# Two decode layers on one core: FFN weights packed at the turn, column sums moved, kept scores split with ScalarE, outputs scaled on ScalarE, y copied in parts

## The chip, the core and the metric

One core of a Trainium2 chip runs the whole program. Its engines run side by side, each its own instructions in order: TensorE (PE), VectorE (DVE), ScalarE (ACT) and GpSimd (POOL). SyncE (SP) only issues loads from the chip's main memory into the on-chip arena. PE writes its results to a small memory of its own, from which DVE and ACT read. The metric is device time in microseconds (us); lower is better.

## What is computed

Two equal layers, each attention over a long cache and then a gated FFN, for two sequences and one new token each. D = 448, 16 heads of 256, 4096 cached keys, F = 1792, all float32:

```python
def _A_ref(x, k_cache, v_cache, wq, wo):
    q = (x @ wq).reshape(B, Sq, H, Dh).transpose(0, 2, 1, 3)
    scores = einsum("bhqd,bhkd->bhqk", q, k_cache) * (Dh ** -0.5)
    o = einsum("bhqk,bhkd->bhqd", softmax(scores), v_cache)
    return o.transpose(0, 2, 1, 3).reshape(B, Sq, H * Dh) @ wo
def _B_ref(x, W_gate, W_up, W_down):
    gate = x @ W_gate
    return (gate * (gate > 0) * (x @ W_up)) @ W_down

x = A_x
x = x + _A_ref(_layernorm(x), k_cache, v_cache, wq, wo)
x = x + _B_ref(_layernorm(x), W_gate, W_up, W_down)
x = x + _A_ref(_layernorm(x), k_cache, v_cache, wq, wo)
x = x + _B_ref(_layernorm(x), W_gate, W_up, W_down)
```

Both layers use the same weights and the same cache. Nearly all the work is reading keys and values: 32 pairs of head and sequence, each with 4 MiB of keys and 4 MiB of values, in each layer.

## The kernel before

**Units.** A unit `u` is one pair of head and sequence; 32 of them make an attention. Its 4096 keys lie as 32 tiles of 256 columns over 128 partitions, loaded in up to four chunks of eight tiles (1 MiB). The main loop of `attention` goes over `u` and handles the scores of unit `u`, the weighting of values of unit `u - 1`, and the output of unit `u - 2`, in an order that is written out by hand; nothing reorders it. So each engine has one fixed list of instructions.

**Scores** (`score`, `score_block`). Where a unit's keys came in one piece, DVE multiplies all 32 tiles by the query in one instruction (L378) and sums each tile in another (L386). In units 25 to 28 of the first layer and 25 to 29 of the second, ACT sums the first eight tiles (L382) and DVE the other 24. Where keys came in chunks, DVE and ACT share them chunk by chunk (L409, L411, L415), or DVE multiplies and sums one tile in one fused instruction (L418). Then POOL finds the maximum over the partitions (L429), ACT takes the exponentials (L434, L437).

**Values and output.** `weigh` (L462) is 16 PE matmuls for a unit. `out_copy` (ACT, L475) and `out_add` (DVE, L478) fold the result, `out_turn` (PE, L488) turns it, `out_keep` (DVE, L501) divides it by the softmax sums, for both sequences of a head at once in odd units, and `project` (PE, L511) multiplies by wo. On DVE, `out_keep` of unit `u - 2` stands behind three of the four chunks of the scores of unit `u`. The scoring query of a new head (`query`, L309 to L342) stands on PE behind `project`.

**Kept keys.** The second layer goes through the heads in another order and begins with the last two heads of the first. The keys of units 29, 30 and 31 of the first layer, and the values of 30 and 31, are therefore loaded once and kept: their scores in the first layer may not overwrite them, so L418 writes its products to a tile that nobody reads, `junk` (part of `down`). ACT has no part in them.

**Loads.** The arena holds 27 units of 1 MiB: three blocks of eight, and three singles for weights. `pump` issues the loads of a list, `pending`, strictly in order on SP, as soon as a place is free; `release` frees a place and calls `pump`. A load of a list that has no place holds back all behind it. SP waits with each for the engines that used the place last, and for the eighth load before it.

**The turn.** Between the two attentions lies `ffn(False)`: `absorb` adds the attention's result to x, `proj` multiplies by the seven pieces of w_in (L576; pieces 0 to 3 for the gate, 3 to 6 for the other half), `block` by the four of w_out (L669). Each piece of w_in has 1792 columns and takes a unit of 2048. Between pieces 4 and 5, PE computes column sums of the next query weights (`between`, L596 to L606) for the next layer's first query, which is put together without waiting for the layernorm. `busy` issues matmuls that nobody reads, so that PE isn't idle in short waits; `FILL` says where. `ffn(True)` is the same at the end, with the output y gathered in PE's memory (`y_left`, and `y_end` for the last 64 columns), copied at L702 and L710, and sent by SP (L703) and ACT (L711).

Of the kernel before, what the change touches and what calls it, by code (L numbers as in the profile page):

```python
# [15 lines left out]
P = 128  # L16
# [7 lines left out]
PAIR = 2 * NC  # L24
WHOLE_FIRST = range(1, 28)
WHOLE_SECOND = range(9, 29)
KEPT = 20
ALONE = 25
# [11 lines left out]
class Arena:  # L40


    def __init__(self):
        self.free = set(range(BLOCKS * PAIR + SINGLES))

    def take(self, n, kind, after=None):


        split = {}
        for size in (2, NC, PAIR):  # L50
            for i in range(0, BLOCKS * PAIR, size):
                if all(k in self.free for k in range(i, i + size)):
                    split |= {k: size for k in range(i, i + size)}
        found = sorted(self.free, key=lambda k: (split.get(k, 1), k))
# [11 lines left out]
        self.free -= set(range(found[0], found[0] + n))  # L66
# [4 lines left out]
def two_layers(  # L71
# [20 lines left out]
    arena = consts.tile([P, (BLOCKS * PAIR + SINGLES) * UNIT], F32, name="arena")  # L92
# [9 lines left out]
    def source(key, n):  # L102
# [6 lines left out]
        if kind == "h":  # L109
            return w_head[name]  # L110
        if kind == "in":
            return w_in[c]
        return w_out[:, 14 * P * c : min(14 * P * (c + 1), 14 * D)]

    def pump():
        while pending:
            (kind, name, c), n = pending[0]
            last = at_of.get((kind, name, c - 1)) if kind in "kv" else None
            at = units.take(n, kind, last)
            if at is None:  # L120
                return
            pending.pop(0)
            src = source((kind, name, c), n)
            dst = arena[:, at * UNIT : at * UNIT + src.shape[1]]
# [7 lines left out]
            for k in range(n):  # L132
# [3 lines left out]
                at_of[key] = at + k  # L136
# [3 lines left out]
    def get(*key):  # L140
        at = at_of[key]
        return arena[:, at * UNIT : (at + 1) * UNIT]

    def release(*key):
        units.free.add(at_of.pop(key))
        pump()
# [46 lines left out]
    pending += of_first + [(key, 1) for key in ffn_loads]  # L193
# [4 lines left out]
    junk = down[:, :DH]  # L198
    y_end_row = row[SUMS : SUMS + B, D:]
# [41 lines left out]
    def busy(n):  # L241
# [6 lines left out]
        )  # L248

# [45 lines left out]
    def attention(order, after, q_first=None, begun=None):  # L295
# [74 lines left out]
        def score_block(u, c):  # L370


            at = at_of["k", order[u], 0] * UNIT
# [5 lines left out]
            shared = 0 if (WHOLE_SECOND if ahead else WHOLE_FIRST)[0] <= u < ALONE else CT  # L379
# [11 lines left out]
        def score(u, c):  # L391
# [24 lines left out]
            else:  # L416
                for t in range(whole, CT):
                    nc.vector.scalar_tensor_tensor(  # L418
# [26 lines left out]
        def softmax_sum(u):  # L445
# [4 lines left out]
            nc.vector.reciprocal(r_of[u - 1], total)  # L450

        def weigh(u, c):
# [3 lines left out]
            if (u - n_u, c) in FILL:  # L456
# [37 lines left out]

        def out_keep(u):
            if u % 2 == 0:
                return
            h = order[u][0]
            oT_of[h] = work.tile([P, 2, B], F32, name="oT")
            share = r_of.pop(u - 1)[:, None, :].to_broadcast([P, 2, B])  # L500
            nc.vector.tensor_mul(oT_of[h], pT_of.pop(u - 1), share)  # L501
# [58 lines left out]
    def ffn(last):  # L560
# [5 lines left out]
        if not last:  # L566
            h, b = second[0]
            w_q = get("h", h, 0)

        def proj(parts):  # L570

            p = ps_f.tile([P, D], F32, name="pf")
            for n, (part, c, done) in enumerate(parts):
                w = get("in", "", part)
                for j in range(4):
                    nc.tensor.matmul(  # L576
                        p[32 * j : 32 * j + 32, :],
                        xs[:, c, :32],
                        w[:, j * D : (j + 1) * D],
# [3 lines left out]
                if done:  # L583
                    release("in", "", part)
                if part in (4, 5):
# [3 lines left out]
        def between(part):  # L589
# [4 lines left out]
            elif part == 4:  # L594
                for c in range(2):
                    nc.tensor.matmul(  # L596
                        cols, ones.to_broadcast([P, P]), w_q[:, c * DH : (c + 1) * DH],
                        start=(c == 0), stop=False,
                    )
            else:  # L600
                nc.tensor.matmul(
                    cols, ones.to_broadcast([P, P]), w_q[:, 2 * DH : FULL * DH],
                    start=False, stop=False,
                )
                for j in range(2):
                    nc.tensor.matmul(  # L606
                        cols[:, j * P : (j + 1) * P],
# [227 lines left out]
```

## Time and profile before

| | |
|---|---|
| median of 3 runs | 1320.69 us (1320.47 to 1320.93) |
| the profiled execution: its own time | 1320.27 us |
| its span | 1318.5 us |
| loads | 562.56 MB, 427 GB/s over the span |
| busy: DVE, PE, POOL, ACT | 82%, 42%, 20%, 15% |
| mean clock that PE was granted | 0.68 |

The span goes from the first to the last instruction of the profiled execution; 1.8 us of its time lie around it. Rows of a timeline begin with the start (us from the span's start) and the duration, then engine, line, operation and operands; in brackets stands how long the engine sat idle before and what ended that. In rows of groups, "x51 | 443.3, 8692" is 51 instructions, 443.3 us together and 8692 ns each. SPq and ACTq are the queues that issue transfers. Line numbers are those of the kernel before unless a row names the changed one.

### The profile page before, as it was taken

The page shows a single profiled execution, that of the slowest core. Times are in us where ns is not written, and L with a number is a line of the kernel's source. Part 1 is how long each engine was busy: PE and PEld are TensorE (multiplying, and loading weights), DVE is VectorE, ACT ScalarE, POOL GpSimd, SP SyncE. Part 2 cuts the span into 40 slices and gives each one's busy share as a digit, 9 for nine tenths or more (in the row PEclk, how much of TensorE's full clock was granted, in tenths as well). Part 3 has the DMA queues.
Part 4 walks back from the last instruction along what each step waited for, and adds up shares of the span by engine and source line. Part 5 has one row for each costly group of instructions (what it writes and reads, how often), then busy time and mean ns, then how long its engine had stood idle before and what let it go on. Part 6 is the DMA issues. An engine that isn't in the chain of part 4 may idle for free.

```text
span 1318.5 us, 9085 instructions
## 1 busy us (share of the span) xinstructions
PE 553.7 (42%) x3276; PEld 190.6 (14%) x3276; DVE 1081.6 (82%) x780; ACT 195.6 (15%) x776; POOL 269.0 (20%) x192
## 2 busy tenths in 40 slices
PE   2243342433434324345585444242433424434348
PEld 2011010110111101112141111110111101101113
DVE  4989888898888988888729987798888988877892
ACT  2100000000000000212026513000000000012241
POOL 0002003322133220321001153030123331230210
PEclk9675666656667667666697777666767667666679
DMA  9999999999999999999999999999999999999998
GB/s 408 435 430 429 432 428 437 432 436 434 417 445 435 430 430 426 445 418 430 421 405 416 431 430 435 438 432 430 432 431 436 433 428 436 429 432 425 427 425 334
DMA packets 22665, 563.16 MB, mean 427 GB/s; under 512 B 2520, under 2 KB 2652, under 8 KB 9564
## 3 DMA queue, kind: packets, MB, share of 16 engines
q1 hardware_dynamic: 22612, 562.57, 99.5%
q8 instruction: 26, 0.43, 0.1%
q14 instruction: 19, 0.16, 0.0%
q10 hardware_dynamic: 8, 0.00, 0.0%
HBM read 562.56 MB, written 0.00 MB: 427 GB/s over the span
## 4 chain that ended last, share of the span: by engine, by line
DMA 55%; DVE 32%; PE 7%; POOL 2%; issue 2%; ACT 1%; DVEq 0%; SPq 0%; POOLq 0%; ACTq 0%
DMA arena<-in_vk_dram 54%; DVE arena L378 12%; DVE scores L386 11%; DVE arena L409 3%; DVE down L418 2%; PE po L462 2%; POOL top L429 2%; DVE arena L418 2%; DMA arena<-in_w_out_dram 1%; DVE row L478 1%; PE small L488 1%; PE acc L511 1%; DVE scores L415 1%; ACT arena L411 1%; PE pf L576 1%
## 5 line engine op out<-in xcount | busy, mean ns | idle before, releaser
L378 DVE TENSOR_TENSOR arena<-arena 128x8192 f32<-128x8192 f32 x51 | 443.3, 8692 | 111.0 <-DMA arena<-in_vk_dram 110.9
L386 DVE TENSOR_REDUCE scores<-arena 128x32 f32<-128x8192 f32 (+1 forms) x53 | 431.8, 8148 | 0.0
L488 PE MATMUL small<-ones,row 128*128 128x1 f32 x256 | 62.0, 346 | 686.3 <-DVE row L478 686.3
L462 PE MATMUL po<-arena,probs 128*2 128x512 f32 x2048 | 303.1, 734 | 10.3 <-DMA arena<-in_vk_dram 6.6
L429 POOL PARTITION_ALL_REDUCE top<-mx x64 | 64.6, 1009 | 645.8 <-DVE mx L427 645.8
L443 POOL PARTITION_ALL_REDUCE total<-rs x64 | 176.1, 2752 | 61.3 <-ACT probs L437 60.3
L488 PEld LDWEIGHTS small<-ones,row 128*128 128x128 f32 x256 | 56.5, 308 | 748.9 <-DVE row L478 748.9
L434 ACT ACTIVATE nm<-top,nsr 128x1 f32<-128x1 f32 x64 | 18.8, 294 | 612.4 <-POOL top L429 612.4
L354 POOL PARTITION_BROADCAST arena<-arena x58 | 27.6, 545 | 300.6 <-ACT arena L350 300.6
L462 PEld LDWEIGHTS po<-arena,probs 128*2 128x2 f32 x2048 | 54.8, 96 | 198.3 <-issue 191.2
L338 PE MATMUL pq<-arena,xs 128*33 128x256 f32 x174 | 70.6, 571 | 14.1 <-DMA arena<-in_w_head_dram 14.1
L511 PE MATMUL acc<-arena,oT 128*2 128x448 f32 x128 | 50.9, 894 | 32.1 <-DVE oT L501 32.1
L350 ACT ACTIVATE arena<-pq 33x256 f32<-33x256 f32 x29 | 10.9, 377 | 321.7 <-PE pq L342 321.7
L382 ACT ACTIVATE arena<-arena 128x256 f32<-128x256 f32 x104 | 41.7, 402 | 86.2 <-DVE arena L378 86.2
L478 DVE SCALAR_TENSOR_TENSOR row<-po,lead,row 128x256 f32<-128x256 f32 x64 | 30.7, 479 | 25.8 <-ACT row L475 25.4
L411 ACT ACTIVATE arena<-arena 128x256 f32<-128x256 f32 x117 | 47.1, 404 | 20.4 <-DVE arena L409 20.1
L409 DVE TENSOR_TENSOR arena<-arena 128x1024 f32<-128x1024 f32 (+1 forms) x24 | 42.0, 1748 | 0.0
L338 PEld LDWEIGHTS pq<-arena,xs 128*33 128x33 f32 x174 | 25.3, 162 | 81.3 <-issue 66.7
L475 ACT ACTIVATE row<-po,lead 128x256 f32<-128x256 f32 x64 | 29.1, 455 | 21.2 <-PE po L462 21.2
L418 DVE SCALAR_TENSOR_TENSOR down<-arena,pq 128x256 f32<-128x256 f32 x64 | 26.9, 420 | 5.4 <-DMA arena<-in_vk_dram 3.4
L501 DVE TENSOR_TENSOR oT<-small,ri 128x4 f32<-128x4 f32 x32 | 5.1, 161 | 29.0 <-PE small L488 29.0
L437 ACT ACTIVATE probs<-scores,nm,sr 128x32 f32<-128x32 f32 x64 | 26.4, 413 | 2.1
(145 smaller groups left out, 359.0 us busy)
## 6 DMA issues: line engine op xcount, KB each, us to landing
arena<-in_vk_dram SPq DMA_DIRECT2D x16, 4096.0 KB, 40.0
arena<-in_w_head_dram SPq DMA_DIRECT2D x31, 896.0 KB, 30.9
arena<-in_vk_dram SPq DMA_DIRECT2D x27, 1024.0 KB, 14.9
arena<-in_vk_dram SPq DMA_DIRECT2D x12, 2048.0 KB, 38.5
arena<-in_w_in_dram SPq DMA_DIRECT2D x14, 896.0 KB, 26.2
arena<-in_w_out_dram SPq DMA_DIRECT2D x5, 896.0 KB, 8.9
arena<-in_vk_dram SPq DMA_DIRECT2D x47, 43.4
arena<-in_w_out_dram SPq DMA_DIRECT2D x1, 512.0 KB, 17.3
```

Source lines behind the costliest of these rows:

```text
L338: nc.tensor.matmul(q, xs[:, c, :], w[:, c * DH : (c + 1) * DH], start=(c == 0), stop=False)
L378: nc.vector.tensor_mul(kt, kt, q_of[u][:, None, :].to_broadcast([P, NT, DH]))
L386: nc.vector.reduce_sum(s_of[u][:, shared:], kt[:, shared:, :], axis=AX.X)
L409: nc.vector.tensor_mul(some, some, q_of[u][:, None, :].to_broadcast([P, whole, DH]))
L411: nc.scalar.activation(kt[:, t, :], kt[:, t, :], AF.Copy, accum_out=found[:, t : t + 1])
L418: nc.vector.scalar_tensor_tensor(junk if kept else kt[:, t, :], kt[:, t, :], 1.0, q_of[u], op0=ALU.mult, op1=ALU.mult, accum_out=found[:, ...
L429: nc.gpsimd.partition_all_reduce(mx_of[u], mx, P, RED.max)
L443: nc.gpsimd.partition_all_reduce(total[:, b : b + 1], rs, P, RED.add)
L462: nc.tensor.matmul(po_of[u][32 * t : 32 * t + 2, :], p_of[u][:, n : n + 2], vt[:, 2 * t * DH : (2 * t + 2) * DH], start=(c == 0), stop=(c ...
L478: nc.vector.scalar_tensor_tensor(row[:, :DH], po_of.pop(u)[:, DH:], lead[:, 1:2], row[:, :DH], op0=ALU.mult, op1=ALU.add,)
L488: nc.tensor.matmul(pT_of[u - u % 2][:, c, b : b + 1], row[:, c * P : (c + 1) * P], ones, start=True, stop=True,)
L511: nc.tensor.matmul(acc[at : at + B], oT_of[h][:, c, :], wo[:, c * D : (c + 1) * D], start=(n < 3), stop=(n >= n_u - 3),)
```

## The change

Six things, in the diff below:

- **Places at the turn.** Free space is now counted in cells of 64 columns, 32 to a unit, and one cell is added between the singles and the blocks. The 11 FFN loads of the turn get fixed places from a table, `TURN`, back to back over two singles and three units of the first block; the other loads are placed as before. Piece 5 of w_in is loaded in two parts, of 1344 and 448 columns; the second ("in", 7) goes where piece 0 was.
- **Column sums** of the next query weights are taken on PE before the last unit's first and last values (`columns`), in place of two `busy` fillers, and are scaled later, by way of `share`.
- **ALONE is gone**: DVE sums all 32 tiles in every block from the first whole one on.
- **Kept scores**: every odd tile is multiplied on DVE into one buffer, `product` (half of `row`), and summed on ACT, which writes in the same place; even tiles stay fused on DVE.
- **Output scaling** goes from DVE (one instruction for two units) to ACT (`out_scale`, one for each unit).
- **y in parts**: at the end 256 columns of y are copied on DVE before the last block, the next 128 on ACT from a tile of their own (`y_third`).

Some small tiles also take names of others (`nm`, `top`, `mx`, `rs`) and so share their buffers.

```diff
+CELL = 64
+UC = UNIT // CELL
+GAP = 1
+LAYER = 28
+TURN = {
+    ("in", 0): (1, 0, LAYER), ("in", 1): (3, 12, LAYER), ("in", 2): (4, 8, LAYER),
+    ("in", 3): (5, 4, LAYER), ("in", 4): (1, 28, LAYER), ("in", 5): (2, 24, 21),
+    ("in", 7): (1, 0, 7), ("in", 6): (3, 12, LAYER), ("out", 0): (4, 8, LAYER),
+    ("out", 1): (5, 4, LAYER), ("out", 2): (1, 28, LAYER), ("out", 3): (1, 7, 14),
+}
-ALONE = 25
...
+            packed = kind in ("in", "out") and len(pending) > len(ffn_loads)
+            src = source((kind, name, c), n, packed)
+            if packed:
+                unit, skip, size = TURN[kind, c]
+                start = unit * UC + skip + GAP * (unit >= SINGLES)
+                if not units.claim(start, size):
+                    return
...
+    def columns(c):
+        w_q = get("h", second[0][0], 0)
+        if c == 0:
+            cols_of.append(ps_f.tile([P, DH], F32, name="pf"))
+            for i in range(2):
+                nc.tensor.matmul(
+                    cols_of[0], ones.to_broadcast([P, P]), w_q[:, i * DH : (i + 1) * DH],
+                    start=(i == 0), stop=False,
+                )
+            return
...
-            shared = 0 if (WHOLE_SECOND if ahead else WHOLE_FIRST)[0] <= u < ALONE else CT
+            shared = 0 if u >= (WHOLE_SECOND if ahead else WHOLE_FIRST)[0] else CT
...
                 for t in range(whole, CT):
+                    if kept and t % 2:
+                        nc.vector.tensor_mul(product, kt[:, t, :], q_of[u])
+                        nc.scalar.activation(
+                            product, product, AF.Copy, accum_out=found[:, t : t + 1]
+                        )
+                        continue
                     nc.vector.scalar_tensor_tensor(
...
+            oT_of[order[u][0]] = work.tile([P, 2, B], F32, name="oT")
+            out_scale(u - 1)
...
-            if (u - n_u, c) in FILL:
+            if u == n_u - 1 and after and c in (0, NC - 1):
+                columns(c)
+            elif (u - n_u, c) in FILL:
                 busy(FILL[u - n_u, c])
...
+        def out_scale(u):
+            h, b = order[u]
+            share = r_of[u - u % 2][:, b : b + 1]
+            nc.scalar.activation(oT_of[h][:, :, b], pT_of[u - u % 2][:, :, b], AF.Copy, scale=share)
+
         def out_keep(u):
-            if u % 2 == 0:
-                return
-            h = order[u][0]
-            oT_of[h] = work.tile([P, 2, B], F32, name="oT")
-            share = r_of.pop(u - 1)[:, None, :].to_broadcast([P, 2, B])
-            nc.vector.tensor_mul(oT_of[h], pT_of.pop(u - 1), share)
+            if u % 2:
+                out_scale(u)
...
+            turn_cols = w_q[:, FULL * DH + P + 2 * D :]
+            nc.scalar.activation(turn_cols, cols_of.pop(), AF.Copy)
...
-            nc.tensor.matmul(y_left, unit, left, start=True, stop=False)
+            nc.tensor.matmul(y_left[:, : 2 * P], unit, left[:, : 2 * P], start=True, stop=False)
+            y_third = ps_s.tile([P, P], F32, name="small")[SUMS : SUMS + B]
+            nc.tensor.matmul(y_third, unit, left[:, 2 * P :], start=True, stop=False)
...
+            nc.vector.tensor_copy(left[:, : 2 * P], y_left[:, : 2 * P])
             at = block(pds[FULL], FULL, range(14 - CLOSE))
             nc.scalar.activation(down[:, at], pds[FULL][:, at], AF.Copy)
-            to_y(before, True)
-            nc.vector.tensor_copy(left, y_left)
+            nc.tensor.matmul(y_third, scaled, down[:, before], start=False, stop=True)
+            nc.scalar.activation(left[:, before], y_third, AF.Copy)
             nc.sync.dma_start(found[:, : FULL * P], left)
```

Three places show what this does to the engines' lists. In the rows, waits stand in brackets by the engine (or load lane, DMAHW) that is waited for, `arena` holds the keys, `row` the product buffer and `down` the tile that nobody reads.

DVE before, from the last block's reduction (unit 28, first layer) into the first kept unit, 29:

```order
L386 TENSOR_REDUCE scores<-arena 128x24
L427 TENSOR_REDUCE mx<-scores 128x1
L418 SCALAR_TENSOR_TENSOR down,scores<-arena 128x256 x8
L478 SCALAR_TENSOR_TENSOR row<-po,lead,row 128x256
L418 SCALAR_TENSOR_TENSOR down,scores<-arena 128x256 x16
L501 TENSOR_TENSOR oT<-small,ri 128x4
```

and DVE of the changed kernel at the same place:

```order
L450 TENSOR_REDUCE scores<-arena 128x32 [waits DVE_49]
L497 TENSOR_REDUCE mx<-scores 128x1 [waits DVE_49]
L488 SCALAR_TENSOR_TENSOR down,scores<-arena 128x256 [waits DMAHW6_49]
L483 TENSOR_TENSOR row<-arena 128x256
L488 SCALAR_TENSOR_TENSOR down,scores<-arena 128x256 [waits DVE_49]
L483 TENSOR_TENSOR row<-arena 128x256 [waits Activation_49]
```

The reduction has all 32 tiles, the run of fused tiles became pairs, and from its second on each multiply into `row` waits for ACT; the scaling (oT) has left the list.

ACT of the changed kernel, from the softmax of unit 28 through unit 29 (nm and probs are the softmax, `row<-po` the output copy of unit 27, `row,scores<-row` the sums of the products, oT the scaling of unit 27); before, nothing stood between `row<-po` and the next nm:

```order
L504 ACTIVATE nm<-top,nsr 128x1 [waits Pool_49]
L507 ACTIVATE probs,rs<-scores,nm,sr 128x32 [waits DVE_49,Activation_49]
L549 ACTIVATE row<-po,lead 128x256 [waits PE_49]
L484 ACTIVATE row,scores<-row 128x256 [waits DVE_49] x12
L572 ACTIVATE oT<-small,ri 128x2 [waits PE_49]
L484 ACTIVATE row,scores<-row 128x256 [waits DVE_49] x4
```

The sums stand behind an output copy that waits for PE, and the scaling, for which PE's projection waits, behind twelve of them.

SP before, from piece 4 of w_in to the first of w_out:

```order
L131 DMA arena<-in_w_in_dram 128x1792 [waits DVE_49,DMAHW6_49,PE_49,Pool_49]
L131 DMA arena<-in_w_in_dram 128x1792 [waits DMAHW7_49,DMAHW2_49,PE_49]
L131 DMA arena<-in_w_in_dram 128x1792 [waits DMAHW3_49,DMAHW0_49,PE_49]
L131 DMA arena<-in_w_out_dram 128x1792 [waits DMAHW4_49,DMAHW1_49,PE_49]
L131 DMA arena<-in_w_out_dram 128x1792 [waits DMAHW5_49,PE_49]
```

and SP of the changed kernel:

```order
L166 DMA arena<-in_w_in_dram 128x1792 [waits DVE_49,DMAHW6_49,PE_49,Pool_49]
L166 DMA arena<-in_w_in_dram 128x1344 [waits DMAHW7_49]
L166 DMA arena<-in_w_in_dram 128x448 [waits DMAHW2_49,DMAHW0_49,PE_49]
L166 DMA arena<-in_w_in_dram 128x1792 [waits DMAHW3_49,DMAHW1_49,PE_49]
L166 DMA arena<-in_w_out_dram 128x1792 [waits DMAHW4_49,PE_49]
```

The larger part of piece 5 waits for no engine of its own any more, only for a load lane; the smaller part and piece 6 wait for PE, as pieces 5 and 6 did.

113 lines of the change are left out of this document (65 added, 48 removed).

## The prediction

> **What bounds the kernel now.** I read the page's row of bytes moved, then two-microsecond windows around the turn between the two layers, then the SP queue's own timeline there, and last the timelines of PE, DVE and ACT. The columns of a window row are its bounds and length, busy time (and count) of PE, weight load, DVE, ACT and POOL, the granted clock, DMA share and GB/s.
>
> ```profile
> GB/s 408 435 430 429 432 428 437 432 436 434 417 445 435 430 430 426 445 418 430 421 405 416 431 430 435 438 432 430 432 431 436 433 428 436 429 432 425 427 425 334
> q1 hardware_dynamic: 22612, 562.57, 99.5%
> 668.00:670.00 2.00, 1.91 (x24) 0.77 (x26) 0.94 (x6) 0.02 (x1) 0.00 (x0) 1.00 0.74 308
> 670.00:672.00 2.00, 2.00 (x21) 0.47 (x14) 0.00 (x0) 0.00 (x0) 0.00 (x0) 1.00 0.85 287
> 652.29 0.33 SPq L131 DMA_DIRECT2D arena<-in_w_in_dram  x1
> 669.46 1.08 SPq L131 DMA_DIRECT2D arena<-in_w_in_dram  x2
> ```
>
> Loads fill 99.5% of the span at some 430 GB/s, so only three things can move the end: a hole in the loads, a rate, and the tail behind the last load. The one hole inside is the turn. Against about 420 GB/s (the slice before the turn has 421), the two windows lack (112 + 133) x 2 / 420 = 1.2 us. The SP rows say why: the fifth piece of w_in goes out at 652.29, the next two only at 669.46, once the first FFN matmuls have freed a place. So **the start of the first FFN sets when loads go on**, and the chain to it is this:
>
> ```profile
> 615.24 1.66 PE L511 MATMUL acc<-arena,oT 128*2 128x448 f32 x4 [6.41 <-DVE oT L501]
> 649.27 0.91 PE L511 MATMUL acc<-arena,oT 128*2 128x448 f32 x2 [6.34 <-DVE oT L501]
> PEld po L462 <- DMA arena<-in_vk_dram: 1.0, 1, 1.0
> 603.57 0.19 DVE L427 TENSOR_REDUCE mx<-scores 128x1 f32<-128x32 f32 x1
> 603.67 0.41 DVE L418 SCALAR_TENSOR_TENSOR down<-arena 128x256 f32<-128x256 f32 x1
> 604.13 0.42 DVE L418 SCALAR_TENSOR_TENSOR down<-arena 128x256 f32<-128x256 f32 x1
> 622.41 0.42 DVE L418 SCALAR_TENSOR_TENSOR down<-arena,pq 128x256 f32<-128x256 f32 x1 [3.36 <-DMA arena<-in_vk_dram]
> 637.70 0.19 DVE L427 TENSOR_REDUCE mx<-scores 128x1 f32<-128x32 f32 x1
> 637.80 0.41 DVE L418 SCALAR_TENSOR_TENSOR down<-arena,pq 128x256 f32<-128x256 f32 x1
> ```
>
> Units 29, 30 and 31 (the kept ones) start their scores on DVE at 603.67, 622.41 and 637.80. PE's projections of units 26/27 (615.24) and 28/29 (649.27) wait for the output scaling that stands on DVE behind 24 of the 32 tiles of units 29 and 31. Unit 30 waits for its query, which PE computes behind the first of them (622.41 - 615.24 = 7.2 us; the page names a load there, but the query matmuls ended just before). From 649.27 to the FFN, PE waits for a load once, 1.0 us. DVE's 50 us from 603.67 on thus carry the turn, with 1.0 us to spare.
>
> **Part 1: score blocks lose ACT's eight tiles** (units 25 to 28 of the first layer, 25 to 29 of the second).
>
> ```profile
> L386 DVE TENSOR_REDUCE scores<-arena 128x32 f32<-128x8192 f32 x40 | 346.8, 8671 | 0.0
> L386 DVE TENSOR_REDUCE scores<-arena 128x24 f32<-128x6144 f32 x13 | 85.0, 6538 | 0.0
> 577.86 0.48 DVE L478 SCALAR_TENSOR_TENSOR row<-po,lead,row 128x256 f32<-128x256 f32 x1
> 579.44 0.16 DVE L501 TENSOR_TENSOR oT<-small,ri 128x4 f32<-128x4 f32 x1 [1.10 <-PE small L488]
> 579.52 6.54 DVE L386 TENSOR_REDUCE scores<-arena 128x24 f32<-128x6144 f32 x1
> ```
>
> A reduction of 32 tiles costs 8.67 - 6.54 = 2.13 us more. Units 25 and 26 give it back in DVE's later waits for loads; 27 and 28 follow each other without one: +4.26. **Part 2, output scaling to ACT**, takes the step at 579.44 and its wait for PE out of DVE: the reduction can start some 1.2 us earlier. DVE reaches unit 29 at +4.26 - 1.2 = **+3.1**. ACT pays some 0.2 us per unit, mostly idle there.
>
> **Part 3: kept tiles in pairs.** The old form runs every 0.46 us (603.67, 604.13), 0.93 a pair. Now DVE fuses the even tile, multiplies the odd one into a single buffer, and ACT sums that; the next multiply waits for ACT. No row shows a 256-wide multiply; it lies on the line of the wider ones:
>
> ```profile
> L409 DVE TENSOR_TENSOR arena<-arena 128x2048 f32<-128x2048 f32 x12 | 27.4, 2281 | 0.0
> L409 DVE TENSOR_TENSOR arena<-arena,pf 128x768 f32<-128x768 f32 x3 | 2.8, 949 | 0.0
> 688.62 0.42 DVE L418 SCALAR_TENSOR_TENSOR arena<-arena,pf 128x256 f32<-128x256 f32 x1 [0.66 <-PE pf L725]
> 688.96 0.41 DVE L418 SCALAR_TENSOR_TENSOR arena<-arena,pf 128x256 f32<-128x256 f32 x1
> 1270.05 0.40 ACT L411 ACTIVATE arena<-arena 128x256 f32<-128x256 f32 x1
> 1270.36 0.19 ACT L411 ACTIVATION_READ_ACCUMULATOR arena<-arena 128x1 f32 x1
> 1270.58 0.19 DVE L427 TENSOR_REDUCE mx<-scores 128x1 f32<-128x32 f32 x1 [0.52 <-ACT arena L411]
> ```
>
> (2281 - 949) / 1280 = 1.04 ns an element, so 949 - 512 x 1.04 = 0.41 us. ACT's sum with its accumulator read takes 1270.55 - 1270.05 = 0.50, and DVE goes on 0.03 later. The loop from one odd multiply to the next is 0.41 + 0.04 + 0.50 + 0.04 = **0.99 us**, the even tile inside it. Bounds: if the loop never bit, DVE alone would need 0.34 (688.62 to 688.96, no wait on itself) + 0.41 = 0.75; with 0.05 more at each hand-over, 1.1. I take 0.99, since each piece is a row.
>
> The Trainium skill, "VectorE: DVE Perf Modes", section "The DRAIN you can't avoid", says that a semaphore between chained DVE operations costs nothing extra. The trace disagrees: the same 256-wide instruction repeats after 0.46 us where it waits for its own predecessor and after 0.34 where it doesn't. By the page the fused tile would keep 0.46, no pair could be under 0.87, and the result could not lie under about 1328.
>
> ACT works in order, so a unit's first product waits for the softmax and the output copy before it:
>
> ```profile
> 605.07 0.45 ACT L475 ACTIVATE row<-po,lead 128x256 f32<-128x256 f32 x1
> 625.68 0.47 ACT L475 ACTIVATE row<-po,lead 128x256 f32<-128x256 f32 x1 [5.24 <-PE po L462]
> ```
>
> Unit 29: ACT is free 605.52 - 603.67 = 1.85 after the unit's start, sums for 0.50, so tile 3's multiply starts at 2.4; ten loops to tile 23 are 9.9, its end 0.95, the scaling 0.2: 13.45 to the projection, where it was 11.6: **+1.9**. Unit 30: ACT is held until 626.15, 3.75 after the start, by the output copy that waits for PE; 4.3 + 14 loops 13.9 + 0.95 = 19.1 to the maximum, where it was 15.3: **+3.8**. Unit 31 like 29, where it was 11.5: **+2.0**. Altogether the projection of 28/29 comes 3.1 + 1.9 + 3.8 + 2.0 = **10.8 us later**; in general 34 loops less 22.9. Queued behind it on PE are the last two weightings, then the FFN.
>
> **Part 4: column sums** go from the FFN to the last weighting. Taken off the FFN, they free nothing while loads are full. Where they go, they took the place of filler matmuls in the 1.0 us wait for values, which is gone now. This row gives the larger half, 1.1 us, an upper bound; the filler it replaces is the lower one, 0. I take **+0.6**.
>
> ```profile
> 674.48 1.13 PE L596 MATMUL pq<-arena,ones 128*128 128x256 f32 x4
> arena<-in_w_in_dram SPq DMA_DIRECT2D x14, 896.0 KB, 26.2
> ```
>
> **Part 5: packing.** Bytes stay; three quarters of piece 5 (672 KB, 1.6 us at 420 GB/s) can be queued before the FFN. The extra request costs nothing visible beside full queues. With the FFN 10.8 - 1.0 + 0.6 = 10.4 late, the hole is 1.2 + 10.4 - 1.6 = 10.0: **+8.8 us**. Lost load time is never made up.
>
> **Part 6: the end.**
>
> ```profile
> 1220.97 8.69 DVE L378 TENSOR_TENSOR arena<-arena 128x8192 f32<-128x8192 f32 x1 [4.51 <-DMA arena<-in_vk_dram]
> 1248.53 0.16 DVE L501 TENSOR_TENSOR oT<-small,ri 128x4 f32<-128x4 f32 x1 [1.11 <-PE small L488]
> 1281.73 0.15 DVE L501 TENSOR_TENSOR oT<-small,ri 128x4 f32<-128x4 f32 x1
> 1312.10 0.96 PE L669 MATMUL pf<-arena,row 128*32 128x128 f32 x26 [0.17 <-DMA arena<-in_w_out_dram]
> 1314.17 0.52 PE L669 MATMUL po<-arena,row 128*32 128x128 f32 x10 [0.30 <-DMA arena<-in_w_out_dram]
> 1314.98 0.47 PE L669 MATMUL pf<-arena,row 128*32 128x64 f32 x18 [0.17 <-DMA arena<-in_w_out_dram]
> 1315.67 0.56 DVE L702 COPY down<-acc 2x384 f32<-2x384 f32 x1 [4.33 <-PE acc L690]
> 1316.26 0.33 SPq L703 DMA_DIRECT2D out_dram<-down  x1
> 1316.49 0.26 ACTq L711 DMA_DIRECT2D out_dram<-row  x1
> ```
>
> DVE waits for a load last at 1220.97 (unit 28). Units 28 and 29 cost 4.26, less 1.2 for the wait at 1248.53: +3.1. The last but one scaling, now on ACT behind its four tiles, comes some 0.5 later. PE's waits for w_out, 0.17 + 0.30 + 0.17 = 0.64, absorb the first of it. Copying y in parts shortens 0.56, but the ACT request at 1316.49 bounds the gain at about 0.2. Sum 3.1 + 0.5 - 0.6 - 0.2 = **+2.8**.
>
> **Sum.** 8.8 + 2.8 = +11.6. The profiled execution took 1320.27 us, its span 1318.5; the median shown is 1320.69. So 1331.9 beside the profiled run, **1332** beside the median.
>
> **Rivals.** (a) *Sharing pays*: ACT runs ahead and DVE alone sets 0.75 a pair. Then 34 x 0.75 - 22.9 = 2.6 late, a hole of 1.2 + 2.6 - 0.4 - 1.6 = 1.8: +0.6, and with the end 1324. For it speaks that ACT is idle beside the kept units; against it the single buffer. The Trainium skill, "Perfetto Trace Analysis", section "Optimizing Scalar/DVE Operations", says that moving work from a saturated DVE to ScalarE may make sense; the rows above show DVE saturated there, and what that could win is this case. (b) *The hole closes, not slower*: at 0.70 a pair or less, PE's 1.0 us of waiting and the 1.6 us queued ahead swallow all of the delay, and packing takes back the 1.2: with the end 1322, and 1319.5 if the w_out loads set the end after all. It decides only at or below 0.70, under the 0.75 of DVE's own rows. (c) *Packing doesn't come through*: piece 5 stands on SP behind piece 4, which waits for a head's weights that the late projection frees; if both come too late, the 1.6 are lost too: 1334.
>
> **Chances.** Forecast with (c) 0.68, its own range 1328 (loop 0.87) to 1338 (loop 1.1 and (c)); (a) 0.12; (b) 0.14; something that I don't see and that makes it faster 0.06, since all the gains found, 1.2 + 0.6 + 0.2, stay under 0.2%, the 2.6 us that measuring this kernel tells from no change. So faster 0.06, same 0.14, slower 0.80. The range takes in (a) and the middle of (b): 1321 to 1338.
>
> **What would show it.** Right: products on ACT 0.99 us apart and DVE waiting for ACT; the projection of 28/29 near 660; windows without loads for some 10 us near 670 to 680; DVE's last load wait still at unit 28. Wrong: pairs at 0.75, no DVE wait for ACT, loads without a hole, or the last scores no later against the last loads.

## The result and the profile after

| | before | changed |
|---|---|---|
| median | 1320.69 us (1320.47 to 1321.08, 5 runs) | 1333.17 us (1332.93 to 1333.84, 5 runs) |
| span of the profiled execution | 1318.5 us | 1331.1 us |
| loads, mean | 427 GB/s | 423 GB/s |

The changed kernel is slower: the ratio is 1.0095, with a 95% interval of 1.0081 to 1.011. That is 12.5 us; the forecast was 11.6 by its sum, at 1332.

First the two-microsecond windows of the changed kernel around the turn (columns as in the prediction's windows; the last is GB/s):

```profile
670.00:672.00 2.00, 2.00 (x19) 0.43 (x11) 0.00 (x0) 0.00 (x0) 0.00 (x0) 1.00 0.75 310
672.00:674.00 2.00, 2.00 (x15) 1.10 (x16) 0.00 (x0) 0.00 (x0) 0.00 (x0) 1.00 0.30 122
674.00:676.00 2.00, 1.73 (x12) 0.61 (x6) 0.48 (x1) 0.67 (x2) 0.00 (x0) 1.00 0.02 8
676.00:678.00 2.00, 1.76 (x9) 0.50 (x9) 0.00 (x0) 0.96 (x4) 0.00 (x0) 1.00 0.00 0
678.00:680.00 2.00, 1.91 (x22) 1.36 (x25) 1.52 (x10) 1.28 (x1) 0.00 (x0) 1.00 0.00 0
680.00:682.00 2.00, 2.00 (x27) 0.78 (x20) 0.12 (x1) 0.00 (x0) 0.00 (x0) 1.00 0.20 47
682.00:684.00 2.00, 2.00 (x16) 0.63 (x12) 0.00 (x0) 0.25 (x2) 0.00 (x0) 1.00 0.78 194
```

Against 420 GB/s these seven windows lack (110 + 298 + 412 + 420 + 420 + 373 + 226) x 2 / 420 = 10.8 us of loads, where the kernel before lacked 1.2. The requests on SP's queue frame the hole: piece 4 of w_in and the larger part of piece 5 go out from 661.11 on, the next two only from 680.38, behind the first FFN matmuls:

```profile
661.11 0.80 SPq L166 DMA_DIRECT2D arena<-in_w_in_dram  x2
...
680.38 1.70 SPq L166 DMA_DIRECT2D arena<-in_w_in_dram  x2
```

Now the timelines of DVE, ACT and PE ahead of it. Row L488 is the fused form, L483 the multiply into the single buffer, L484 ACT's sum of it, L586 the projection, L657 the first FFN matmuls:

```profile
606.56 0.41 DVE L488 SCALAR_TENSOR_TENSOR down<-arena 128x256 f32<-128x256 f32 x1
...
608.84 0.42 DVE L483 TENSOR_TENSOR row<-arena 128x256 f32<-128x256 f32 x1 [1.18 <-ACT row L484]
...
609.30 0.42 ACT L484 ACTIVATE row<-row 128x256 f32<-128x256 f32 x1 [0.49 <-DVE row L483]
...
609.62 0.19 ACT L484 ACTIVATION_READ_ACCUMULATOR row<-row 128x1 f32 x1
...
609.84 0.42 DVE L483 TENSOR_TENSOR row<-arena 128x256 f32<-128x256 f32 x1 [0.23 <-ACT row L484]
...
620.08 1.66 PE L586 MATMUL acc<-arena,oT 128*2 128x448 f32 x4 [7.29 <-ACT oT L572]
...
626.33 0.42 DVE L488 SCALAR_TENSOR_TENSOR down<-arena,pq 128x256 f32<-128x256 f32 x1 [2.23 <-PE pq L381]
...
630.80 0.42 DVE L483 TENSOR_TENSOR row<-arena,pq 128x256 f32<-128x256 f32 x1 [3.38 <-ACT row L484]
...
645.91 0.41 DVE L488 SCALAR_TENSOR_TENSOR down<-arena,pq 128x256 f32<-128x256 f32 x1
...
659.36 0.91 PE L586 MATMUL acc<-arena,oT 128*2 128x448 f32 x2 [7.25 <-ACT oT L572]
...
679.43 3.21 PE L657 MATMUL pf<-arena,xs 128*32 128x448 f32 x32
```

The last of these rows in the kernel before:

```profile
668.45 3.40 PE L576 MATMUL pf<-arena,xs 128*32 128x448 f32 x32
```

From a unit's second on, each multiply waits for ACT's sum of the one before (DVE mostly sits idle for 0.23 us of it), and the loop repeats after 609.84 - 608.84 = 1.00 us. Unit 29 starts 2.9 us later than before, the two projections 4.8 and 10.1, the first FFN matmuls 679.43 - 668.45 = 11.0. The end, in the timelines of DVE, ACT, PE and the two queues:

```profile
1230.40 8.69 DVE L442 TENSOR_TENSOR arena<-arena 128x8192 f32<-128x8192 f32 x1 [3.72 <-DMA arena<-in_vk_dram]
...
1294.07 0.40 ACT L475 ACTIVATE arena<-arena 128x256 f32<-128x256 f32 x1
...
1294.47 0.24 ACT L572 ACTIVATE oT<-small,ri 128x2 f32<-128x2 f32 x1
...
1294.76 0.91 PE L586 MATMUL acc<-arena,oT 128*2 128x448 f32 x2 [6.52 <-ACT oT L572]
...
1298.05 0.19 DVE L497 TENSOR_REDUCE mx<-scores 128x1 f32<-128x32 f32 x1 [0.52 <-ACT arena L475]
...
1328.15 0.32 SPq L766 DMA_DIRECT2D out_dram<-down  x1
...
1328.67 0.25 ACTq L774 DMA_DIRECT2D out_dram<-row  x1
```

DVE's last wait for a load moved from 1220.97 to 1230.40, by 9.4 us: that is what the turn cost. From there to the end of the span it is 100.7 us, where it was 97.5: 3.2 more. 9.4 + 3.2 = 12.6, the difference of the spans.

### The profile page after: what moved, and what is told of

The parts are those of the page before. It is cut to its first block, busy times and chain, and to the rows that moved or that the text cites. A ratio compares the mean times of both kernels' runs of the same rounds, so it can differ in the third digit from the quotient of the medians.

```text
span 1331.1 us, 9001 instructions
## 1 busy us (share of the span) xinstructions
PE 576.5 (43%) x3274; PEld 193.7 (15%) x3274; DVE 1091.6 (82%) x701; ACT 206.9 (16%) x793; POOL 276.9 (21%) x192
## 4 chain that ended last, share of the span: by engine, by line
DMA 53%; DVE 26%; PE 11%; POOL 4%; ACT 3%; issue 2%; DVEq 0%; SPq 0%; POOLq 0%; ACTq 0%
DMA arena<-in_vk_dram 50%; DVE arena L442 11%; DVE scores L450 9%; POOL top L499 4%; PE po L536 4%; DVE arena L473 2%; DMA arena<-in_w_head_dram 2%; PE pq L402 2%; PE acc L586 2%; ACT row L484 1%; DVE row L483 1%; DVE row L552 1%; ACT arena L475 1%; PE pf L657 1%; PE small L562 1%
## 5 line engine op out<-in xcount | busy, mean ns | idle before, releaser
L450 DVE TENSOR_REDUCE scores<-arena 128x32 f32<-128x8192 f32 (+1 forms) x53 | 451.0, 8510 | 0.0
L536 PE MATMUL po<-arena,probs 128*2 128x512 f32 x2048 | 321.5, 773 | 3.3 <-ACT probs L507 3.3
L499 POOL PARTITION_ALL_REDUCE top<-mx x64 | 71.9, 1123 | 647.4 <-DVE mx L497 647.3
L572 ACT ACTIVATE oT<-small,ri 128x2 f32<-128x2 f32 x64 | 16.6, 259 | 516.2 <-PE small L562 516.2
L402 PE MATMUL pq<-arena,xs 128*33 128x256 f32 x174 | 73.5, 587 | 15.1 <-DMA arena<-in_w_head_dram 15.1
L586 PE MATMUL acc<-arena,oT 128*2 128x448 f32 x128 | 50.9, 892 | 39.3 <-ACT oT L572 39.2
L475 ACT ACTIVATE arena<-arena 128x256 f32<-128x256 f32 x117 | 47.1, 404 | 20.8 <-DVE arena L473 20.6
L406 PE MATMUL pq<-arena,xs 128*33 128x128 f32 x116 | 25.0, 356 | 0.0
L484 ACT ACTIVATE row<-row 128x256 f32<-128x256 f32 x48 | 20.0, 416 | 21.7 <-DVE row L483 21.7
```

Of the source, the lines that this page charges most:

```text
L402: nc.tensor.matmul(q, xs[:, c, :], w[:, c * DH : (c + 1) * DH], start=(c == 0), stop=False)
L450: nc.vector.reduce_sum(s_of[u][:, shared:], kt[:, shared:, :], axis=AX.X)
L475: nc.scalar.activation(kt[:, t, :], kt[:, t, :], AF.Copy, accum_out=found[:, t : t + 1])
L484: nc.scalar.activation(product, product, AF.Copy, accum_out=found[:, t : t + 1])
L499: nc.gpsimd.partition_all_reduce(mx_of[u], mx, P, RED.max)
L536: nc.tensor.matmul(po_of[u][32 * t : 32 * t + 2, :], p_of[u][:, n : n + 2], vt[:, 2 * t * DH : (2 * t + 2) * DH], start=(c == 0), stop=(c ...
```

## The experiments

Twelve kernels ran in three groups, each beside the kernel before. The times are medians; the one before had 1320.62, 1320.69 and 1320.77 in the three groups.

| kernel | us | ratio to before, 95% |
|---|---|---|
| changed, ACT's eight tiles back in the late blocks | 1329.54 | 1.0053 to 1.0083 |
| changed, kept keys fused on DVE again | 1324.30 | 1.0018 to 1.0037 |
| changed, two product buffers | 1324.50 | 1.0017 to 1.0040 |
| changed, both score edits undone | 1322.66 | 1.0011 to 1.0030 |
| before, packing alone | 1320.94 | 0.9993 to 1.0010 |
| before, two unread buffers | 1320.58 | 0.9991 to 1.0009 |
| before, packing and two unread buffers | 1320.94 | 0.9992 to 1.0010 |
| changed, scaling back on DVE | 1333.03 | 1.0080 to 1.0107 |
| changed, no packing | 1336.77 | 1.0096 to 1.0125 |
| before, scaling on ACT alone | 1322.41 | 1.0000 to 1.0018 |
| changed, column sums and y as before | 1332.36 | 1.0075 to 1.0103 |
| before, a packing with two cut pieces | 1322.18 | 1.0002 to 1.0019 |

### The kept keys

**Fused form again.** The six lines of the shared odd tiles are taken out:

```diff
-                    if kept and t % 2:
-                        nc.vector.tensor_mul(product, kt[:, t, :], q_of[u])
-                        nc.scalar.activation(
-                            product, product, AF.Copy, accum_out=found[:, t : t + 1]
-                        )
-                        continue
```

> The changed kernel, with the kept keys in the fused form on DVE alone again, nothing of them on ACT. My theory: the projection of units 28/29 comes 2.0 + 4.2 + 2.0 = 8.2 us earlier than 659.36, thus near 651, the first FFN matmuls near 671; the hole falls from 10.8 to about 2.6 and the end does not change: 1325.0. Rival (the hole is due to the late blocks alone): 1333.

Measured: 1324.30, which is 8.9 less, by the theory's 1325.0. The first FFN matmuls come at 669.72:

```profile
669.72 3.21 PE L651 MATMUL pf<-arena,xs 128*32 128x448 f32 x32
```

The projection comes at 642.70, earlier than the 651 expected: it no longer stands behind ACT's sums, nor, as in the kernel before, behind DVE's tiles. What is left against the kernel before lies mostly at the end: DVE's last wait for a load ends at 1221.64, only 0.7 us later, and from there to the end of the span it is 100.7 us, as in the changed kernel, where it was 97.5.

**Two product buffers.** The sharing stays, but odd tiles go to two buffers in turn:

```diff
-    product = row[:, DH:]
+    products = [row[:, DH:], arena[:, LAYER * CELL : UC * CELL]]
...
+                        product = products[t // 2 % 2]
                         nc.vector.tensor_mul(product, kt[:, t, :], q_of[u])
```

> The changed kernel, with two product buffers in turn instead of one; the sharing with ACT stays. My theory (the price of sharing is the single buffer: each multiply waits for ACT's sum of the one before): the loop falls from 0.995 to what DVE alone needs, two starts 0.34 apart, 0.68 a pair; units 29 and 31 gain 4.5 each, unit 30 5.4, the projection of 28/29 comes near 645, the first FFN matmuls near 665, before the place of the kernel before (668.4), and the hole closes: 1333.2 - 10.8 = 1322.4, the end's 2.8 remain. Rival (ACT's sums slow DVE's multiplies, or ACT's queue sets the pace): loop of 0.85 or more, 1328 and up.

Measured: 1324.50, 2.1 more than the theory and far under the rival. DVE's multiplies in this kernel's timeline, with the fused tile between each two:

```profile
612.37 0.42 DVE L484 TENSOR_TENSOR row<-arena 128x256 f32<-128x256 f32 x1
...
612.71 0.42 DVE L489 SCALAR_TENSOR_TENSOR down<-arena 128x256 f32<-128x256 f32 x1
...
613.05 0.42 DVE L484 TENSOR_TENSOR arena<-arena 128x256 f32<-128x256 f32 x1
...
648.39 0.91 PE L587 MATMUL acc<-arena,oT 128*2 128x448 f32 x2 [4.99 <-ACT oT L573]
...
662.69 1.04 PE L537 MATMUL po<-arena,probs 128*2 128x512 f32 x8 [0.37 <-DMA arena<-in_vk_dram]
...
669.12 1.33 PE L658 MATMUL pf<-arena,xs 128*32 128x448 f32 x12
```

The loop is 613.05 - 612.37 = 0.68 us, without a wait in these rows: the single buffer was the price of sharing, as the theory had it. The projection came at 648.39, 11.0 earlier than in the changed kernel, yet the first FFN matmuls stayed at 669.12, where 665 was expected. The fifth row says why: the last weighting waits for values that land just before 662.7. So there is a floor under the start of the FFN that DVE doesn't set.

**Two unread buffers, in the kernel before.** This looks at the fused form by itself:

```diff
-    junk = down[:, :DH]
+    junk = [down[:, :DH], row[:, DH:]]
...
-                        junk if kept else kt[:, t, :], kt[:, t, :], 1.0, q_of[u],
+                        junk[t % 2] if kept else kt[:, t, :], kt[:, t, :], 1.0, q_of[u],
```

> The kernel before, with the kept keys' products written to two unread buffers in turn instead of one. Theory: the fused form then repeats every 0.34 us instead of 0.46, since it no longer waits for its own predecessor's write, the projection of 28/29 comes some 9 us earlier, near 640, and the time still does not move (1320.6), because PE then waits for the values that land near 662. Rival (DVE alone sets the first FFN): FFN near 660, the hole closed, 1319.4. Rival (the 0.46 is not due to the buffer): pitch and projection unchanged.

Measured: 1320.58, no change. DVE's and PE's timelines:

```profile
604.46 0.42 DVE L418 SCALAR_TENSOR_TENSOR down<-arena 128x256 f32<-128x256 f32 x1
...
604.80 0.42 DVE L418 SCALAR_TENSOR_TENSOR row<-arena 128x256 f32<-128x256 f32 x1
...
622.46 0.42 DVE L418 SCALAR_TENSOR_TENSOR down<-arena,pq 128x256 f32<-128x256 f32 x1 [6.86 <-DMA arena<-in_vk_dram]
...
637.90 0.42 DVE L418 SCALAR_TENSOR_TENSOR down<-arena,pq 128x256 f32<-128x256 f32 x1 [3.75 <-DMA arena<-in_vk_dram]
...
646.71 1.66 PE L511 MATMUL acc<-arena,oT 128*2 128x448 f32 x4 [4.93 <-DVE oT L501]
...
662.50 1.04 PE L462 MATMUL po<-arena,probs 128*2 128x512 f32 x8 [0.61 <-DMA arena<-in_vk_dram]
...
668.84 3.39 PE L576 MATMUL pf<-arena,xs 128*32 128x448 f32 x32
```

The fused form now repeats every 0.34 us instead of 0.46. Only its target changed, so it had waited for its own predecessor's write. But the projection moved by 2.6 us, not by the 9 expected, because units 30 and 31 start at 622.46 and 637.90 all the same, with DVE idle for 6.9 and 3.8 us ahead of them. Their keys arrive only then. And the FFN starts no earlier, since the last values land near 662.5. DVE, which I had named as what carries the turn, was thus only level with the loads.

### The late blocks and the output scaling

**ACT's eight tiles back.** In `score_block`:

```diff
+ALONE = 25
...
-            shared = 0 if u >= (WHOLE_SECOND if ahead else WHOLE_FIRST)[0] else CT
+            shared = 0 if (WHOLE_SECOND if ahead else WHOLE_FIRST)[0] <= u < ALONE else CT
```

> The changed kernel, with ACT summing eight tiles of the late score blocks again. My theory (a chain on DVE sets the start of the FFN, a late FFN is a hole in the loads of the same length, and behind the last load DVE's chain runs on to the end): unit 29 starts 4.3 us earlier, near 602.3; the first FFN matmuls (L657 there) near 675.2 instead of 679.43, the hole 4.2 shorter; at the end 3 more: 1333.2 - 4.2 - 3 = 1326. Rival (lost load time is made up later, so that only the end counts): 1330. Rival (the kept units' loop on ACT sets the pace whatever DVE's start is): 1333.

Measured: 1329.54, 3.6 less instead of 7, near the first rival's 1330, but not for its reason: the FFN moved by only 0.9, and most of what was won came at the end.

**Both score edits undone.** The two edits above together.

> The changed kernel with both score edits undone (ACT's eight tiles back in the late blocks, kept keys fused on DVE); packing, scaling on ACT, column sums in the wait and y in parts stay. My theory: the first FFN matmuls near 668, the hole closed by packing (1.2 less than before), the end 0 to 0.5 earlier than before: 1319.3. Rival (packing or the scaling on ACT costs something of its own): 1321 or more.

Measured: 1322.66 (1321.37 to 1326.75); the rival was right, something else in the change costs about 2 us. The traces of both kernels show the same new waits. First DVE's and PE's timelines with the eight tiles back, then ACT, PE and DVE with both edits undone:

```profile
587.10 8.78 DVE L443 TENSOR_TENSOR arena<-arena 128x8192 f32<-128x8192 f32 x1 [2.20 <-POOL arena L419]
...
678.53 3.21 PE L658 MATMUL pf<-arena,xs 128*32 128x448 f32 x32
```

```profile
1249.75 0.40 ACT L447 ACTIVATE arena<-arena 128x256 f32<-128x256 f32 x1
...
1250.15 0.24 ACT L567 ACTIVATE oT<-small,ri 128x2 f32<-128x2 f32 x1
...
1250.44 1.66 PE L581 MATMUL acc<-arena,oT 128*2 128x448 f32 x4 [1.81 <-ACT oT L567]
...
1256.71 2.38 DVE L474 TENSOR_TENSOR arena<-arena 128x2048 f32<-128x2048 f32 x1 [2.40 <-POOL arena L419]
```

ACT sums eight tiles (the last at 1249.75) and only then scales the output, while PE idles 1.8 us for it. The projection, the next head's query behind it on PE and POOL's broadcast of that query are late in turn, and DVE waits 2.4 us before unit 30. The wait of 1.1 us that was taken from DVE came back as one of 2.4. Where the blocks are DVE's alone, as in the changed kernel, ACT is free at that moment and the wait isn't there. So the scaling on ACT suits only blocks that are DVE's alone.

**Scaling on ACT, in the kernel before.** The scaling of `out_keep` is moved as in the change, nothing else:

```diff
...
-            share = r_of.pop(u - 1)[:, None, :].to_broadcast([P, 2, B])
-            nc.vector.tensor_mul(oT_of[h], pT_of.pop(u - 1), share)
+            if u % 2:
+                out_scale(u)
...
```

> The kernel before with the output scaling on ACT alone. The prediction's term: DVE saves its wait of 1.1 to 1.2 us in units 27 and 29, so no loss: 1320.2. Theory by the run with both score edits undone: in the late blocks ACT sums eight tiles first, the scaling stands behind them, the projection and with it the next head's query come some 2.5 us late, DVE waits for POOL's broadcast before unit 28 of the first layer and 30 of the second (2.4 us there), and the last scaling comes behind four more sums: 1322.6.

Measured: 1322.41, by the theory, though the interval of its ratio just reaches 1. In its trace DVE waits for POOL's broadcast for 2.56 us before unit 28 of the first layer (587.53) and 1.61 before unit 30 of the second (1257.24); the kernel before has neither wait.

**Scaling back on DVE, in the changed kernel.** The reverse.

> The changed kernel with the output scaling back on DVE, for both sequences at once. Theory by the rows: DVE waits 1.1 us for PE again in units 27 (first layer) and 29 (second), so unit 29 of the first layer starts 1.1 later, but the projections no longer stand behind ACT's sums, 0.5 to 0.6 each: FFN about 0.1 to 0.6 later, the end within 0.5 of what it is: 1333.5. Rival (the prediction's term, scaling on ACT a plain gain of 1.2 at each place): 1335.4.

Measured: 1333.03 against 1333.17, no difference. In the changed kernel the move is worth nothing either way: the 1.1 us that DVE saves in unit 29 of the second layer are given back at the end, where the last but one scaling stands behind four sums (1294.07 and 1294.47 above). With the scaling on DVE the last maximum comes 1.35 us later after DVE's last load, and the end 1.7 sooner after that.

### Packing

**Packing alone, in the kernel before.** All other parts of the change are undone, but for the later scaling of the column sums and the shared buffers of small tiles.

> The kernel before with packing of w_in alone. Theory: the first FFN matmuls stay near 668.4, since the last values land near 662.1 whatever DVE does; the loads run out 1.6 us later, but the next pieces go out as late as before, so 0.5 to 0.7 of the hole's 1.2 us go: 1320.1. Rival (the prediction's term): all 1.2 go, 1319.5. Rival (more requests and late places cost something): 1321 or more.

**Packing and two unread buffers.**

> The kernel before with packing and two unread buffers, nothing else of the change. Theory: like packing alone, 1320.1, within 0.2 of it. Rival (a place freed earlier lets packing close the whole hole): 1319.4.

Measured: 1320.94 both times, no gain, where the theory had 1320.1. The windows of the kernel with packing alone:

```profile
668.00:670.00 2.00, 1.91 (x21) 0.97 (x24) 1.32 (x9) 0.47 (x1) 0.00 (x0) 1.00 0.99 410
670.00:672.00 2.00, 2.00 (x24) 0.59 (x17) 0.00 (x0) 0.00 (x0) 0.00 (x0) 1.00 0.92 338
672.00:674.00 2.00, 2.00 (x16) 0.67 (x15) 0.27 (x2) 0.60 (x2) 0.00 (x0) 1.00 0.98 341
...
676.00:678.00 2.00, 2.00 (x19) 1.10 (x21) 0.00 (x0) 0.00 (x0) 0.00 (x0) 1.00 1.01 388
```

The hole moved by some 2 us, and these four windows still lack (10 + 82 + 79 + 32) x 2 / 420 = 1.0 us. The DMA engines are no longer idle there (shares of 0.92 and 0.98 instead of 0.74 and 0.85), yet move 340 GB/s. In that stretch lie, beside whole pieces, the cut ones, with rows of 5.4 and 1.8 KB for a partition instead of 7.2. That the short rows make the rate is not shown, and one row speaks against it: the changed kernel without packing, further down, has no cut pieces, and behind its hole the engines were busy at a share of 1.00 and moved 330 GB/s:

```profile
686.00:688.00 2.00, 0.07 (x4) 0.00 (x0) 0.00 (x0) 0.00 (x0) 0.00 (x0) 1.00 1.00 330
```

So the cause of the low rate stays open.

**A packing of mine.** The last piece of w_in is cut too, so that the first place to come free takes 28 cells at once:

```diff
-    ("in", 7): (1, 0, 7), ("in", 6): (3, 12, LAYER), ("out", 0): (4, 8, LAYER),
-    ("out", 1): (5, 4, LAYER), ("out", 2): (1, 28, LAYER), ("out", 3): (1, 7, 14),
+    ("in", 7): (1, 0, 7), ("in", 6): (1, 7, 21), ("in", 8): (3, 12, 7), ("out", 0): (4, 8, LAYER),
+    ("out", 1): (5, 4, LAYER), ("out", 2): (1, 28, LAYER), ("out", 3): (3, 19, 14),
...
-    turn_loads = ffn_loads[:6] + [("in", "", 7)] + ffn_loads[6:]
+    turn_loads = ffn_loads[:6] + [("in", "", c) for c in (7, 6, 8)] + ffn_loads[7:]
...
```

> The kernel before with a packing of mine: the last piece of w_in is cut in 21 and 7 cells too, so that the place that the first matmuls free is filled at once (7 + 21 cells) and the next takes the other 7. Theory (packing alone only moved the hole because the first freed place took 0.5 us of loads): the hole of 1.2 us goes, 1319.5. Rival (a hole left behind the shorter requests, as in packing alone): 1320.7.

Measured: 1322.18, slower, and neither theory. Its windows, and a row of SP's queue:

```profile
682.00:684.00 2.00, 1.70 (x32) 1.39 (x32) 0.19 (x1) 0.52 (x4) 0.00 (x0) 1.00 0.38 152
684.00:686.00 2.00, 2.00 (x35) 1.40 (x33) 0.19 (x1) 0.46 (x4) 0.00 (x0) 1.00 0.65 173
```

```profile
683.72 4.06 SPq L169 DMA_DIRECT2D arena<-in_vk_dram  x3
```

The first hole shrank, and a second one of (268 + 247) x 2 / 420 = 2.5 us opened at 682: the second layer's first loads went out at 683.72 instead of 678.52, in the kernel before. By the table of places that is because mine keep units occupied that those loads need whole; no run tests this. A hole closed at one point of a queue in fixed order had only been moved down it.

**No packing, in the changed kernel.** Pieces of w_in in places of their own again.

> The changed kernel without packing. The first FFN matmuls stay near 679.4. The prediction's term: three quarters of a piece, 1.6 us, are no longer queued ahead, so the hole grows from 10.8 to 12.4 and the time to 1334.8. Rival (by the run with packing alone, where the hole only moved: 0.1 us): packing gives nothing here either, since the small rest of the piece is all that the first freed place takes: 1333.3.

Measured: 1336.77, above both expectations, but scattered from 1331.84 to 1338.59 over five runs. The profiled one (1338.59) shows on PE a wait of 3.14 us for w_in that is 0.18 in the changed kernel, and in the windows behind the turn a slow stretch:

```profile
689.21 0.96 PE L654 MATMUL pf<-arena,xs 128*32 128x448 f32 x8 [3.14 <-DMA arena<-in_w_in_dram]
```

```profile
702.00:724.00 22.00, 13.93 (x71) 6.57 (x70) 20.56 (x86) 14.70 (x64) 1.69 (x4) 0.84 0.97 336
```

The same window of the changed kernel:

```profile
702.00:724.00 22.00, 10.07 (x48) 3.34 (x46) 19.39 (x79) 14.36 (x65) 2.72 (x6) 0.73 1.01 418
```

22 us at 336 instead of 418 are 4.3 us. Its hole, over the windows from 668 to 688, lacks 12.6 us of loads, where the changed kernel's lacks 10.8: 1.8 more, near the prediction's 1.6. Together that is 6.1 of the 6.3 us by which DVE's last wait for a load ends later (1236.68 against 1230.40). What slows the loads from 702 on, and why one run of five came out at 1331.84, stays open. So packing shortens the hole where the FFN is late, by this one profile; its worth in time these runs don't give.

### Column sums and y

Both are put back in the changed kernel: the sums between the pieces of w_in (their scaling stays late), y copied at once.

```diff
-            if u == n_u - 1 and after and c in (0, NC - 1):
-                columns(c)
-            elif (u - n_u, c) in FILL:
+            if (u - n_u, c) in FILL:
...
+            else:
+                columns(0 if part == 4 else NC - 1)
...
-            nc.tensor.matmul(y_third, scaled, down[:, before], start=False, stop=True)
-            nc.scalar.activation(left[:, before], y_third, AF.Copy)
+            to_y(before, True)
+            nc.vector.tensor_copy(left, y_left)
```

> The changed kernel with the column sums back between the pieces of w_in and y copied in one piece. Theory: the first FFN matmuls 0.6 to 0.7 earlier (2.1 us of column sums leave the last weighting, 1.4 us of filler come back), near 678.8, the hole shorter by that; y in one piece costs nothing, since the request on ACT's queue ends last: 1332.5. Rival (the copy in parts brings its 0.2 to 0.5): 1332.9.

Measured: 1332.36 (1331.95 to 1333.84), near the theory's 1332.5, though 0.8 us is less than these runs scatter. The profile is that of the slowest of them: from the projection of 28/29 to the first FFN matmuls it has 679.54 - 659.92 = 19.6 us, where the changed kernel has 20.1, but the FFN starts no earlier than there, and not near 678.8.

None of the twelve beats the kernel before. The parts that looked useful (packing, unread buffers in turn) leave its time where it is.

## Why the prediction was right, and where it was not

| step | predicted | measured |
|---|---|---|
| start of unit 29 | +3.1 | 606.56 - 603.67 = +2.9 |
| loop of a kept pair | 0.99 | 1.00 |
| unit 29, start to projection | 13.45 | 620.08 - 606.56 = 13.5 |
| start of unit 30 | +5.0 | 626.33 - 622.41 = +3.9 |
| unit 30, start to the next unit | +3.8 | (645.91 - 626.33) - (637.80 - 622.41) = +4.2 |
| unit 31, start to projection | +2.0 | 13.45, was 11.47: +2.0 |
| projection of 28/29 | +10.8 | 659.36 - 649.27 = +10.1 |
| first FFN matmuls | +10.4 | +11.0 |
| hole | 10.0 | 10.8 |
| end | +2.8 | +3.2 |

The mechanism held: a chain DVE to PE, a late FFN, places that come free late, a hole of loads that nothing makes up (9.6 us more of it, and DVE's last wait for a load 9.4 later), and DVE's chain behind the last load. The largest term, the loop, was made from rows of other shapes and came out to 0.01 us, and undoing it alone gave 8.9 of 12.5 us back. Rival (a) needed 0.75 a pair; DVE alone does 0.68, but only with a second buffer. Rivals (b) and (c) did not occur: 10.8 us of loads were missing, and the larger part of the cut piece was queued before the FFN.

Four steps were off, and partly cancelled, so that the sum came within 1 us owes something to luck.

- **The second projection sets unit 30.** I set aside the page's word that unit 30 waited for a load. It was right as well: with DVE early, the unit still starts at 622.46. Query and load ended level there: the query's matmuls ended 0.3 us ahead of the unit (622.07), and end with it now (626.29). They also end 6.2 us after the projection's start, where it was 6.8. So 0.9 of the delay of 4.8 us was lost on the way.
- **1.0 us to spare on PE.** There was none. In the kernel before, PE issued filler matmuls until the values came, and filler takes its time (1.02 us from 661.06, right ahead of the last values' matmuls at 662.11) whether anything is waited for or not. The column sums came in at +0.67, against my 0.6: between PE's last two turns lie 675.16 - 667.32 = 7.84 us, where it was 664.26 - 657.09 = 7.17. The same values near 662 are a floor: the kernels with two product buffers, with both score edits undone and with two unread buffers wait for them 0.4 to 0.6 us, and their first FFN matmuls come at 668.7 to 669.1. The kernel with the fused form again doesn't wait for them: PE's last long wait there is for DVE's scores of unit 31 (1.56 us, up to 652.73), and with 7.8 us between the last two turns its FFN starts at 669.72.
- **Packing, -1.6.** Alone it is worth nothing (1320.94 against 1320.69), because the hole moves and the loads behind it run at 340 GB/s, not 420; I had put the cost of the extra request at nothing. In the changed kernel the hole was 1.2 + 11.0 - 10.8 = 1.4 shorter than the late FFN would make it, and 1.8 shorter than without packing, so there the term was about right.
- **The end.** DVE's chain gave 2.8 instead of 3.1. The last but one scaling on ACT cost 1.1, not 0.5: from the last maximum to the next turn on PE it was 3.3 us and is 4.4. So the first FFN matmuls came 4.0 us later, counted from DVE's last load. PE's waits for w_out, now gone, took 1.2 of it back, not 0.64, and ACT's last request is 2.75 late (the run with y copied at once has the same 4.4 us from the first matmuls of w_out to that request, so it isn't the copying); from there to the end of the span it was 2.0 us and is 2.4. Copying y in parts brought SP's request forward, to 0.5 ahead of ACT's, which ends last: no gain.

What I had not seen at all is that the late blocks and the output scaling depend on each other. In the changed kernel ACT's eight tiles beside the scaling on ACT bring 3.6 us, half of the 7 that they are worth by DVE's time.

On the fused form: the Trainium skill, "VectorE: DVE Perf Modes", section "The DRAIN you can't avoid", has it, from eight copies, that a semaphore between chained DVE operations costs nothing extra. The run with two unread buffers shows 0.34 against 0.46 us for the same instruction, so here the wait for the predecessor's write costs 0.12. The Trainium skill, "Perfetto Trace Analysis", section "Optimizing Scalar/DVE Operations", says that moving work from a saturated DVE to ScalarE may make sense. With one buffer that cost 9 us in this kernel, with two it gave 0.68 us a pair, as much as two fused tiles of 0.34 on DVE alone.

## What to carry to other kernels

Work shared between two engines through a single buffer ran here at the sum of both engines' latencies (0.46 + 0.54 = 1.00 us a pair), not at the slower one's rate (0.68 with two buffers); count the round trip before moving it. An engine works in order: what is moved to an idle one must also be free at the instant when it is asked, so look at what stands ahead of it there. And before a chain is called the bound, remove its cause once: here the chain on DVE, the query on PE and the loads were level within half a microsecond, and shortening DVE's alone gained nothing.

## What the runs showed of the hardware that was not expected

A fused multiply and sum of 128x256 on DVE starts every 0.34 us with two target buffers and every 0.46 us with one, though nobody reads the target. ACT's copy of 0.42 us with its accumulator read lets DVE go on 0.54 us after its start (609.30 to 609.84). Loads at nearly the same DMA share (0.97 and 1.01) moved 336 and 418 GB/s from 702 to 724 us in two kernels that differ in where w_in lies; the cause is open.
